# Splitting the last output tile into 512, 320, 128 and 64 columns, with the last 64 finished by ScalarE

One core of one Trainium2 chip. The metric is device microseconds (us) of one execution of the whole program, on the slowest core; there is only one core here. Smaller is better.

## The reference, cut to what matters

```python
    x = A_x                                   # 2048 x 1024, bf16
    h = x + _A_ref(_layernorm(x), ...)        # attention with a memory, 4 segments, 32 heads
    h2 = h + _B_ref(_layernorm(h), ...)       # gated MLP; its last step is the product below
    # in _B_ref:
    return jnp.einsum('bsf,fd->bsd', z1 * g, w_out)     # (2048 x 1792) times (1792 x 1024)
```

Only the very last step matters here. The product with `w_out` is made in 16 row tiles of 128 rows. Each tile sums 14 matmuls of 128 x 128 weights into PSUM, the accumulator memory, for each piece of its 1024 columns. It then adds the residual `h` and is stored.

## The kernel before: the parts that matter

The kernel lists its operations, lets a scheduler order them on each engine, and links them with semaphores. TensorE (PE in the profile) keeps the order of the program. `c3` is the product with `w_out` for one row tile:

```python
    def c3(b, tcl, parts):
        tc = 4 * b + tcl
        if parts[0][0] == 0:
            dma(HX[tc % 4][:], out2d[tc * 128:(tc + 1) * 128, :])       # h comes back, long before
        bks = [bank() for x in parts]
        for fc in range(14):
            for bk, (c0, w) in zip(bks, parts):
                mm(bk[:, 0:w], YT[b, fc][:, tcl * 128:(tcl + 1) * 128], WOUT[:, fc, c0:c0 + w], fc == 0, fc == 13)
        for bk, (c0, w) in zip(bks, parts):
            hh = HX[tc % 4][:, c0:c0 + w]
            tt(hh, hh, bk[:, 0:w], ALU.add)                             # VectorE: residual + PSUM
            dma(out2d[tc * 128:(tc + 1) * 128, c0:c0 + w], hh)          # store, issued by SP
    # ...
            for parts in ([((0, 512), (512, 512))] if (b, tcl) != (3, 3) else
                          [((0, 512),), ((512, 384),), ((896, 128),)]):
                c3(b, tcl, parts)
```

The last tile is already cut into 512, 384 and 128 columns, so that little is left to add and store when the last matmul is done.

The softmax here doesn't subtract the row's maximum and nothing guards it: scores larger than these inputs give would overflow.

## Time and profile before

| | before |
|---|---|
| time, first 3 runs, median | 796.82 us (796.44 to 797.57) |
| span of the profiled execution | 794.4 us (794.358 in the trace) |
| TensorE busy | 783.0 us, 99% |
| start of the last 512-column add | 789.02 us |
| from there to the end of the span, "the tail" | 5.34 us |

The *tail* of the last row runs from the start of the last tile's 512-column add to the end of the span. The page prints the span to 0.1 us; I take its end from the trace to a nanosecond. The lines themselves are in the prediction.

### The profile page before, as it was taken

The page shows a single profiled execution, that of the slowest core. Times are in us where ns is not written, and L with a number is a line of the kernel's source. Part 1 is how long each engine was busy: PE and PEld are TensorE (multiplying, and loading weights), DVE is VectorE, ACT ScalarE, POOL GpSimd, SP SyncE. Part 2 cuts the span into 40 slices and gives each one's busy share as a digit, 9 for nine tenths or more (in the row PEclk, how much of TensorE's full clock was granted, in tenths as well). Part 3 has the DMA queues.
Part 4 walks back from the last instruction along what each step waited for, and adds up shares of the span by engine and source line. Part 5 has one row for each costly group of instructions (what it writes and reads, how often), then busy time and mean ns, then how long its engine had stood idle before and what let it go on. Part 6 is the DMA issues. An engine that isn't in the chain of part 4 may idle for free.

```text
span 794.4 us, 11964 instructions
## 1 busy us (share of the span) xinstructions
PE 783.0 (99%) x5273; PEld 321.3 (40%) x4765; DVE 369.4 (47%) x854; ACT 290.6 (37%) x342; POOL 138.7 (17%) x266
## 2 busy tenths in 40 slices
PE   8999999999999999999999999999999999999998
PEld 3455554555554542341322314443244334424433
DVE  6784687868766686804215051132233223322322
ACT  5778887787778852132323323100000000000000
POOL 0454543444433431200001010000000000000000
PEclk9999999999999999999999999999999999999999
DMA  9756612732333657510000116703310530011001
GB/s 282 190 126 160 147 42 67 147 81 54 74 88 95 160 138 210 157 40 1 1 0 1 33 32 156 183 1 78 109 32 1 119 100 1 0 55 59 0 1 53
DMA packets 129526, 65.02 MB, mean 82 GB/s; under 512 B 96576, under 2 KB 121408, under 8 KB 129472
## 3 DMA queue, kind: packets, MB, share of 16 engines
q1 hardware_dynamic: 129472, 64.25, 32.4%
q8 instruction: 39, 0.64, 0.3%
q14 instruction: 15, 0.12, 0.1%
HBM read 32.51 MB, written 8.39 MB: 51 GB/s over the span
## 4 chain that ended last, share of the span: by engine, by line
PE 96%; DVE 2%; issue 1%; ACT 1%; DMA 0%; POOL 0%; SPq 0%
PE ps L327 78%; PE ps L328 15%; PE ps L464 3%; ACT e L473 0%; DMA xin<-in_A_x_dram 0%; DVE stats L570 0%; DVE xin L489 0%; DVE hx L495 0%; DVE pkt L498 0%; ACT hx L587 0%; PE ps L468 0%; DVE oq L495 0%; SPq L516 0%; DVE v L485 0%; ACT hx L585 0%
## 5 line engine op out<-in xcount | busy, mean ns | idle before, releaser
L327 PE MATMUL ps<-wspT,z 128*128 128x512 bf16 x878 | 193.1, 380 | 0.9
L473 ACT ACTIVATE e<-ps 128x2048 bf16<-128x2048 f32 x80 | 149.8, 1873 | 35.1 <-PE ps L464 35.1
L327 PEld LDWEIGHTS ps<-wspT,z 128*128 128x128 bf16 x896 | 87.6, 98 | 106.5 <-issue 1.0
L473 ACT ACTIVATE z<-ps 128x512 bf16<-128x512 f32 x120 | 63.1, 572 | 145.4 <-PE ps L327 140.5
L495 DVE TENSOR_TENSOR tg<-ps,brow 128x512 bf16<-128x512 f32 x56 | 38.7, 691 | 150.0 <-PE ps L327 119.7
L327 PE MATMUL ps<-hnT,win 128*128 128x512 bf16 x438 | 96.7, 379 | 0.5
L700 POOL TENSOR_SCALAR_AFFINE_SELECT e<-e 128x1024 bf16<-128x1024 bf16 (+1 forms) x80 | 77.3, 966 | 112.3 <-ACT e L473 111.9
L328 PE MATMUL ps<-win,hnT 128*128 128x512 bf16 (+1 forms) x381 | 90.0, 344 | 0.5
L570 DVE BATCH_NORM_STATS2 stats<-z 128x6 f32<-128x448 bf16 x64 | 40.1, 627 | 96.8 <-ACT z L473 95.2
L327 PE MATMUL ps<-wout,y 128*128 128x512 bf16 (+2 forms) x243 | 82.5, 367 | 0.0
L328 PE MATMUL ps<-wout,y 128*128 128x512 bf16 x210 | 79.7, 379 | 0.5
L495 DVE TENSOR_TENSOR hx<-hx,ps 128x512 bf16<-128x512 bf16 (+1 forms) x65 | 42.2, 674 | 77.2 <-PE ps L327 76.8
L327 PEld LDWEIGHTS ps<-hnT,win 128*128 128x128 bf16 x448 | 43.8, 98 | 54.2 <-issue 2.0
L327 PE MATMUL ps<-xnT,wq 128*128 128x512 bf16 x250 | 60.3, 381 | 0.4 <-issue 0.2
L327 PE MATMUL ps<-xnT,wk 128*128 128x512 bf16 (+2 forms) x249 | 57.4, 373 | 2.4 <-DVE ra L502 1.9
L327 PE MATMUL ps<-wv,xnT 128*128 128x512 bf16 x239 | 57.2, 380 | 1.4 <-DMA wv<-in_A_wv_dram 0.5
L327 PE MATMUL ps<-wo,oT 128*128 128x512 bf16 x244 | 57.1, 379 | 0.6
L327 PEld LDWEIGHTS ps<-wout,y 128*128 128x128 bf16 x252 | 24.1, 98 | 72.3 <-issue 69.1
L327 PE MATMUL ps<-win,hnT 128*128 128x512 bf16 x122 | 46.3, 380 | 0.0
L327 PEld LDWEIGHTS ps<-win,hnT 128*128 128x128 bf16 x128 | 12.5, 98 | 81.5 <-issue 80.9
L509 POOL TENSOR_SCALAR rs<-mv 128x1 f32<-128x1 f32 x44 | 10.8, 246 | 192.9 <-DVE mv L573 192.9
L327 PEld LDWEIGHTS ps<-v,e 128*128 128x128 bf16 x1280 | 40.1, 96 | 9.8 <-issue 1.7
(72 smaller groups left out, 635.6 us busy)
## 6 DMA issues: line engine op xcount, KB each, us to landing
win<-in_B_w_in_dram SPq DMA_DIRECT2D x6, 1024.0 KB, 5.4
hx<-in_A_x_dram SPq DMA_DIRECT2D x16, 256.0 KB, 3.2
out_dram<-hx SPq DMA_DIRECT2D x16, 256.0 KB, 2.6
hx<-out_dram SPq DMA_DIRECT2D x16, 256.0 KB, 2.7
out_dram<-hx SPq DMA_DIRECT2D x31, 128.0 KB, 1.7
xin<-in_A_x_dram SPq DMA_DIRECT2D x15, 256.0 KB, 5.0
wout<-in_B_w_out_dram SPq DMA_DIRECT2D x2, 1792.0 KB, 11.1
wq<-in_A_wq_dram SPq DMA_DIRECT2D x2, 1024.0 KB, 8.6
```

Of the source, the lines that this page charges most:

```text
L327: return e.matmul(out, lhsT, rhs, start=start, stop=stop)
L328: return e.add_instruction(mybir.InstMatmult(name="I-%d" % (1000000 + o.idx), engine=e.engine, ins=[e.lower_ap(rhs), e.lower_ap(lhsT)], ou ...
L464: G.op(PE, lambda e: e.matmul(o, lhsT, rhs, start=True, stop=True, tile_position=(32 * i, 0)), [lhsT, rhs], [o], n / 2.4 if last else 3.5, ...
L473: G.op(ACT, lambda e: e.activation(o, i, func, scale=scale, **kw), r, [o], ((172 if inps(i) else 224) + n_of(i)) / 1.2 + 26, prio=prio, na ...
L495: G.op(DVE, lambda e: e.tensor_tensor(o, a, b, op), [a, b], [o], vcost(o, [a, b], fast), name="tt", prio=late[0])
L509: G.op(POOL, lambda e: e.tensor_single_scalar(o, i, s, op), [i], [o], 220 if n_of(o) < 8 else 220 + 2.5 * n_of(o), name="pts1", prio=late[0])
L570: G.op(DVE, lambda e, si=si, so=so: e.bn_stats(so, si), [si], [so], (cs + 143) / 0.96, name="bn_stats", prio=late[0])
L700: G.op(POOL, lambda e: e.affine_select(d, d, pat, ALU.is_ge, 0.0, base=0, channel_multiplier=-1), [d], [d], 1270 if j else 640, name="mask")
```

## The change

The intent is a shorter tail. The last piece is halved to 64 columns. Its residual goes into PSUM by a matmul with the identity, so that nothing has to be added afterwards. ScalarE copies it out and issues its store, so that no hand-over to another engine lies between copy and store.

```diff
+    LAST = take("last", [128, 64], BF16)
...
+        last = parts[0][1] == 64
+        if last:
+            mm(bks[0][:, 0:64], IDENT[:], HX[tc % 4][:, 960:1024], True, False)
         for fc in range(14):
             for bk, (c0, w) in zip(bks, parts):
-                mm(bk[:, 0:w], YT[b, fc][:, tcl * 128:(tcl + 1) * 128], WOUT[:, fc, c0:c0 + w], fc == 0, fc == 13)
+                mm(bk[:, 0:w], YT[b, fc][:, tcl * 128:(tcl + 1) * 128], WOUT[:, fc, c0:c0 + w],
+                   fc == 0 and not last, fc == 13)
+        if last:
+            act(LAST[:], bks[0][:, 0:64], ACTF.Copy)
+            dma(out2d[tc * 128:(tc + 1) * 128, 960:1024], LAST[:], eng=ACT)
+            return
...
-                          [((0, 512),), ((512, 384),), ((896, 128),)]):
+                          [((0, 512),), ((512, 320),), ((832, 128),), ((960, 64),)]):
```

## The prediction

> **What bounds the kernel now.** I read the page's busy line and its chain first, to see which engine sets the end:
>
> ```profile
> span 794.4 us, 11964 instructions
> PE 783.0 (99%) x5273; PEld 321.3 (40%) x4765; DVE 369.4 (47%) x854; ACT 290.6 (37%) x342; POOL 138.7 (17%) x266
> ...
> PE 96%; DVE 2%; issue 1%; ACT 1%; DMA 0%; POOL 0%; SPq 0%
> ```
>
> TensorE (PE) is busy for 99% of the span and 96% of the chain that ends last, so the kernel is one unbroken stream of matmuls. The change touches only the last of 16 row tiles of the output, after 785 us. Everything before should stay as it is, so the whole question is the tail. For that I read the timeline from 785 us on, one engine at a time (columns: start us, us, engine, line, operation, count). The vector engine (DVE):
>
> ```profile
> 789.02 0.69 DVE L495 TENSOR_TENSOR hx<-hx,ps 128x512 bf16<-128x512 bf16 x1 [1.95 <-PE ps L327]
> 791.29 0.55 DVE L495 TENSOR_TENSOR hx<-hx,ps 128x384 bf16<-128x384 bf16 x1 [1.58 <-PE ps L327]
> 792.08 0.29 DVE L495 TENSOR_TENSOR hx<-hx,ps 128x128 bf16<-128x128 bf16 x1 [0.23 <-PE ps L327]
> ```
>
> These three adds evict the pieces of 512, 384 and 128 columns; each starts when its piece's fourteenth matmul is done, so their starts are a clock for PE. Next PE's last piece, and the two last store issues of the DMA queue:
>
> ```profile
> 791.09 0.94 PE L327 MATMUL ps<-wout,y 128*128 128x128 bf16 x14
> ```
>
> ```profile
> 791.87 0.33 SPq L516 DMA_DIRECT2D out_dram<-hx  x1
> 792.39 0.33 SPq L516 DMA_DIRECT2D out_dram<-hx  x1
> ```
>
> The DVE add ends at 792.08 + 0.29 = 792.37, its store is issued 0.02 to 0.03 us later, and then nothing runs but that store. Its time to landing is in the list of DMA issues (KB each, us from issue to landing):
>
> ```profile
> out_dram<-hx SPq DMA_DIRECT2D x31, 128.0 KB, 1.7
> ...
> out_dram<-hx SPq DMA_DIRECT2D x1, 96.0 KB, 1.6
> out_dram<-hx SPq DMA_DIRECT2D x1, 32.0 KB, 1.5
> ```
>
> So the last store lands at 792.39 + 1.5 = 793.89, and the remaining 794.36 - 793.89 = 0.47 us (span 794.4) are the end of the program. After PE's last matmul the tail is therefore add 0.29, issue hop 0.03, store 1.5, end 0.47. Of these the change can alter only the first three and when PE finishes.
>
> **What the skill says.** (1) The Trainium skill, "TensorE: Matmul & The Clock Gate", section "Wait — 56ns, not 53.3ns?", gives a warm pitch of N/2.4 ns plus about 2.5 ns, never under about 25 ns. The trace agrees: the fourteen 128-column matmuls above are (0.94 - 0.22)/13 = 55 ns apart (0.22 is one matmul's row), and in the attention part sixteen of 33 columns, each with its own weights, are (0.56 - 0.18)/15 = 25 ns apart:
>
> ```profile
> 299.99 0.56 PE L327 MATMUL ps<-v,e 128*128 128x33 bf16 x16
> ```
>
> (2) "ScalarE: Activation LUTs", section "What ACT_TABLE_LOAD costs", gives an activation with immediate scale and bias 186 ns plus 0.833 ns per column, 239 ns at 64. The trace's PSUM copies are quicker than that (mean ns behind the comma), so I use them:
>
> ```profile
> L473 ACT ACTIVATE qk<-ps 128x256 bf16<-128x256 f32 x16 | 5.3, 383 | 0.0
> ...
> L473 ACT ACTIVATE qk<-ps 128x384 bf16<-128x384 f32 x1 | 0.5, 490 | 1.0 <-PE ps L327 1.0
> L473 ACT ACTIVATE qk<-ps 128x128 bf16<-128x128 f32 x1 | 0.3, 272 | 0.0
> ```
>
> (3) The same page, section "Table sets: the hidden batching unit", says that cheap functions such as copy and identity are in every set. The trace agrees: only three table loads in all, though copies stand among exponentials and GELUs. So I count no table load. (4) "DMA: Bandwidth & Descriptors", section "Issuing engines are not separate DMA queues": a DMA that ScalarE issues runs on the same 16 engines, and issuing elsewhere saves only the sequencer's time. No ScalarE-issued transfer is in this trace, so that term is unverified here.
>
> **The change part by part.**
>
> *PE.* Before, the last tile is 14 x (512, 384, 128). The DVE starts give the pitch at 384: (791.29 - 789.02)/14 = 162 ns, against 160 + 2.5 by the rule; 128 is 55.8 by the rule, in line with the 55 read above. For 320 columns the rule gives 133.3 + 2.5 = 135.8 ns and for 64 columns 26.7 + 2.5 = 29.2 ns. After, the two pieces beyond 512 become three: 14 x (135.8 + 55.8 + 29.2) = 3.09 us plus one identity matmul of 0.03 = 3.12 us; before they take 14 x (162.5 + 55.8) = 3.06 us. Column work is equal, and the 15 additional matmuls cost 14 x 2.5 ns + 29 ns = 0.06 us. All of it is on the path: PE ends 0.06 us later.
>
> *Eviction.* DVE 289 ns at 128 columns is replaced by a ScalarE copy of 64. Its rows fall by (490 - 272)/256 = 0.85 ns per column, so 64 columns cost 272 - 54 = 218 ns: 0.07 us saved. The residual needs no time of its own, as it is in PSUM already. The hand-over from PE costs the same: in the timeline the median from a matmul's modelled end to the start that waited for it is 38 ns on both engines. ScalarE's last work before is over at 503 us, so it is free.
>
> *Issue.* Before: DVE to SP hop 0.03 us. After: the issue on ScalarE waits for its own copy's semaphore, which I also take as 0.03 us. The SP queue still stores the 320 and 128 pieces. The 128 piece's add should start near 791.70, end at 791.99, and its SP issue take 792.02 to 792.35. The ScalarE issue would come at 792.08 + 0.06 + 0.22 + 0.03 = 792.39, just after, so they don't overlap. That is the same moment as the last issue now.
>
> *Store.* 16 KB instead of 32. From 96 to 32 KB the landing time falls from 1.6 to 1.5, about 2 ns per KB, so 16 KB gives 1.47: 0.03 us saved.
>
> *Sum.* +0.06 - 0.07 + 0.00 - 0.03 = -0.04 us. The change trades one thing for another almost exactly. Against it stands a first-time cost of an issue from ScalarE: the first nine loads on the SP queue took a median of 0.43 us to issue against 0.33 at the end, so I allow an estimated +0.1 us. Net +0.06 us on 796.82: 796.9 us.
>
> *What does not move.* The new 128-byte tile fits in the first free region (6400 bytes, of which six 1024-byte tiles took 6144), so the other buffers only shift by 128 bytes and none changes region. The PE order is the program's, and the operations before the last tile keep theirs.
>
> **The rivals.**
>
> *A: the intended gain.* The author counts on a shorter tail: a smaller copy and store, no engine change between copy and issue. At best the issue hop vanishes (-0.03), the store lands in 1.35 (-0.15) and the copy takes 0.19 (-0.10): -0.2 us net of PE, so 796.6. For it: the tail is serial. Against it: landing time hardly depends on size in the rows above (128 KB 1.7, 32 KB 1.5), so halving a small store buys little.
>
> *B: ScalarE's queue is slower.* A DMA issued from an engine that has issued none might take 0.5 us or more to issue, or land later because its queue is fresh. +0.2 to +0.6 us: 797.0 to 797.4. For it: nothing in the profile shows such an issue, and the start of the program shows slower first issues. Against it: the skill's page says the same hardware does it.
>
> *C: small matmuls bound by weight loads.* Each matmul loads its own 128 x 128 weights. If that load set the pace and 64 columns ran at the 55 ns of 128, the last piece would cost 14 x 26 = 0.37 us more: 797.2. Against it: the 33-column run above has a load for each matmul too, and keeps 25 ns. I give it little.
>
> *D: a disturbance elsewhere* through shifted addresses or another schedule order. It would show before 785 us; I see no mechanism.
>
> **Range and chances.** All rivals lie between 796.6 and 797.4, and the three runs before spread from 796.44 to 797.57, more than any of them. So the range is set by run noise: 796.3 to 797.5. Two per cent is 16 us, seven times everything after PE's last matmul (2.3 us), so removing the whole tail wouldn't reach it: within 2% at 0.985.
>
> **What would show it.** Right: the timeline identical up to the last tile; the 320-column add starting near 790.92 and the 128 one near 791.70; fourteen or fifteen 64-column matmuls about 29 ns apart; the ScalarE copy starting near 792.14 and taking about 218 ns; its issue near 792.39; span 794.3 to 794.6. Wrong: a ScalarE issue of over 0.5 us, or starting over 0.1 us after the copy's end (B); a landing under 1.4 us (A); a 64-column pitch above 40 ns (C); a table load before the copy; or any difference before 785 us (D).

## More of the kernel before

At the start of the program, 11 warm-up matmuls on zeros (`N_WARM = 11`) run while the first loads arrive.

The tail leaves out whatever happened in the 789 us before it.

## The result and the profile after

The changed kernel takes 796.41 us (median of 6 runs, 796.05 to 796.88). The kernel before, in the same rounds and the first three runs together, takes 796.72 (796.27 to 797.57). Ratios here are the mean time of one kernel's fast runs over the mean of the other's of the same rounds, so they are not quite the ratio of the medians. This ratio is 0.9994, with a 95% interval from 0.9981 to 1.0007: the same. (A run counts as fast unless it is over 1.5% above the quickest of its kernel. Every run here that has a verdict is fast, those with a short dip of the clock, of which more below, included.)

In the profiled execution the span is 794.7 us, longer than the 794.4 before. The page of the changed kernel, its busy line and its chain:

```profile
span 794.7 us, 11997 instructions
...
PE 783.0 (99%) x5288; PEld 321.9 (41%) x4780; DVE 369.3 (46%) x854; ACT 290.9 (37%) x343; POOL 139.0 (17%) x266
...
PE 95%; DVE 1%; issue 1%; DMA 1%; ACT 1%; SPq 0%; POOL 0%
```

TensorE has the same busy time, 15 matmuls more and 15 weight loads more (PEld, 4780 against 4765): 30 of the 33 instructions that the trace has more are TensorE's, a number to remember. The timeline of the tail, first VectorE, then TensorE, then ScalarE, each in its own fence (start us, us, engine, line, operation, count):

```profile
789.31 0.69 DVE L495 TENSOR_TENSOR hx<-hx,ps 128x512 bf16<-128x512 bf16 x1 [1.95 <-PE ps L327]
791.21 0.49 DVE L495 TENSOR_TENSOR hx<-hx,ps 128x320 bf16<-128x320 bf16 x1 [1.21 <-PE ps L327]
791.99 0.29 DVE L495 TENSOR_TENSOR hx<-hx,ps 128x128 bf16<-128x128 bf16 x1 [0.29 <-PE ps L327]
```

```profile
791.79 0.19 PE L327 MATMUL ps<-hx,ident 128*128 128x64 bf16 x1
791.82 0.57 PE L327 MATMUL ps<-wout,y 128*128 128x64 bf16 x14
```

```profile
792.43 0.22 ACT L473 ACTIVATE last<-ps 128x64 bf16<-128x64 f32 x1 [289.58 <-PE ps L327]
792.68 0.38 ACTq L516 DMA_DIRECT2D out_dram<-last  x1
```

The 512-column add starts 0.29 us later than in the profile before, so 0.29 us were lost before the changed part was reached. Counted from that add, all goes as worked out: the adds at 1.90 and 2.68 us, the 64-column matmuls (0.57 - 0.19)/13 = 29 ns apart, the copy at 3.12 us and of 0.22 us, its store issued at 3.37 us. What was not foreseen is in the stores. (A store is *issued* by SP or ScalarE, which takes some tenths of a microsecond, and it has *landed* when its data have arrived; landing times count from the start of the issue.) SP's last two issues, and then the list of issues of the tail (KB each, us from issue to landing):

```profile
791.72 0.33 SPq L516 DMA_DIRECT2D out_dram<-hx  x1
...
792.31 0.51 SPq L516 DMA_DIRECT2D out_dram<-hx  x1
```

```profile
out_dram<-hx SPq DMA_DIRECT2D x1, 80.0 KB, 1.8
out_dram<-hx SPq DMA_DIRECT2D x1, 32.0 KB, 1.7
out_dram<-last ACTq DMA_DIRECT2D x1, 16.0 KB, 1.5
```

The 128-column store takes 0.51 us to issue instead of 0.33, and the two SP stores land in 1.8 and 1.7 us, where 96 and 32 KB took 1.6 and 1.5 before. ScalarE's store is still the last to land, at 4.91 us after the add, where the last one before landed at 4.86. The tail is 5.39 us, 0.05 longer than before. So three questions: what holds the stores up, why the time nevertheless came out 0.3 us lower, and whether the parts of the change are worth anything by themselves.

### The profile page after: what moved, and what is told of

Its sections match the earlier page's. It is cut to its first block, busy times and chain, and to the rows that moved or that the text cites. A ratio compares the mean times of both kernels' runs of the same rounds, so it can differ in the third digit from the quotient of the medians.

```text
span 794.7 us, 11997 instructions
## 1 busy us (share of the span) xinstructions
PE 783.0 (99%) x5288; PEld 321.9 (41%) x4780; DVE 369.3 (46%) x854; ACT 290.9 (37%) x343; POOL 139.0 (17%) x266
## 4 chain that ended last, share of the span: by engine, by line
PE 95%; DVE 1%; issue 1%; DMA 1%; ACT 1%; SPq 0%; POOL 0%
PE ps L327 78%; PE ps L328 15%; PE ps L464 3%; DMA wv<-in_A_wv_dram 1%; ACT e L473 0%; DVE stats L570 0%; SPq L516 0%; DVE pkt L498 0%; DVE hx L495 0%; DVE xin L489 0%; DVE oq L495 0%; DVE v L485 0%; POOL e L700 0%; POOL ra L505 0%; DVE qk L485 0%
## 5 line engine op out<-in xcount | busy, mean ns | idle before, releaser
L327 PE MATMUL ps<-wout,y 128*128 128x512 bf16 (+3 forms) x257 | 82.5, 356 | 0.0
```

The source lines that it names most:

```text
L327: return e.matmul(out, lhsT, rhs, start=start, stop=stop)
```

## The experiments

Because time can't resolve a tenth of a microsecond here, the tail of the profile is the main measure, and time is a check.

### The kernel before, again

No edit.

> The kernel before against itself. I use the tail, the time from the start of the final tile's 512-column add to the end of the span: 5.34 us in the profile before, 5.39 us in the profile after. Theory N (the 0.3 us between the medians is run noise): the ratio of this identical kernel also strays by up to 0.0010 from 1, its interval includes 1, single runs spread over 1 us, and the tail repeats at 5.34 +- 0.03. Theory R (the change really gains 0.3 us somewhere): the ratio is 1.0000 +- 0.0002, so that 0.9994 stands out from it.

Ratio of the kernel before to itself: 0.9999, interval 0.9985 to 1.0013. Tail 5.35 us. The tail repeats to 0.01 us, while the time does not: one of these 6 runs took 798.34 us, the other five 796.12 to 796.56. In the 11 runs of before beside it, four took 798.08 to 798.50 and seven 795.67 to 796.79. All five long ones have a mean granted clock of 0.998 and all short ones 1.0. So a ratio of 0.9994 is well inside what a kernel does against itself, by the interval. The ratio alone doesn't decide it: 0.9999 is what theory R had expected too.

### The changed kernel, again (twice)

No edit.

> The changed kernel unaltered, more rounds on the same chip as the kernel before against itself. Theory N: ratio within 0.0006 of that other ratio, interval including 1, tail 5.39 +- 0.03, so 0.05 longer than before. Theory R: ratio 0.9993 to 0.9997 with an interval that excludes 1.

Ratio 0.9993, interval 0.9980 to 1.0007, so the interval includes 1. But the tail was 5.75 us, not 5.39 +- 0.03. SP and ScalarE in the timeline of this run, and its issues:

```profile
791.85 0.76 SPq L516 DMA_DIRECT2D out_dram<-hx  x1
...
792.22 0.38 ACTq L516 DMA_DIRECT2D out_dram<-last  x1
```

```profile
out_dram<-hx SPq DMA_DIRECT2D x1, 80.0 KB, 2.1
out_dram<-hx SPq DMA_DIRECT2D x1, 32.0 KB, 2.2
```

Same instructions at the same distances up to SP's last issue, which now takes 0.76 us; the 32 KB store then lands in 2.2 us. My second theory, of a fixed 0.05, fell here. Leaving out the runs with a clock below 1.0, the mean is 796.23 us for five runs of the changed kernel and 796.15 for seven of before on the same chip: the sign turns round. The advantage of the changed kernel in the ratio comes from having had none of the long runs.

A third profile, after the cause below had been formed:

> The changed kernel unaltered, a third profile. Its tail was 5.39 and 5.75 us. Theory F (a race of one instruction fetch with the stores): a fetch at 2.1 to 2.3 us after the 512-column add again, SP's second-last issue again over 0.4 us, tail between 5.38 and 5.85, varying with how long the fetch holds its engine. If the collision were an accident of the first two runs: issue 0.33, tail 5.34.

Tail 5.61 us, SP's last issue 0.86 us. So the hold-up is in all three profiles of the changed kernel, with tails of 5.39, 5.75 and 5.61 us, on average 5.58, which is 0.24 us above before.

### The last store from SP

```diff
-            dma(out2d[tc * 128:(tc + 1) * 128, 960:1024], LAST[:], eng=ACT)
+            dma(out2d[tc * 128:(tc + 1) * 128, 960:1024], LAST[:])
```

> The changed kernel with its last store issued by SP instead of ScalarE. In the changed kernel's profile the SP queue's store of the 128-column piece took 0.51 us to issue where others take 0.33, and landed in 1.7 us where 1.5 was seen. Theory O (the two issues overlap and slow each other): with one queue both issues take 0.33 us, the last store is issued 3.37 us after the 512-column add starts, lands in 1.48 us, and the tail is 5.32 to 5.34 us, 0.05 to 0.07 below the changed kernel. Rival (ScalarE's queue costs nothing, the slow issue was chance): tail 5.39 +- 0.02.

Tail 5.74 us; SP's last two issues take 0.70 and 0.43 us. Neither side was right. There is no ScalarE store here, and the slow issue is still there, so it isn't two queues meeting. Here the slow issue delays the last store directly, which waits behind it on the same queue and is issued 3.75 us after the add instead of 3.37.

### The pieces alone

```diff
-                          [((0, 512),), ((512, 384),), ((896, 128),)]):
+                          [((0, 512),), ((512, 320),), ((832, 128),), ((960, 64),)]):
```

This edit is on the kernel before: no identity matmul, no ScalarE.

> Pieces 512, 320, 128, 64 alone: VectorE adds every residual and SP issues every store, no identity matmul. From the adds of 384 and 128 columns (553 and 289 ns) the 64-column add takes 223 ns, as long as the ScalarE copy, and PE ends 0.03 us sooner. My sum: add starts 3.09 us after the 512-column add, ends 3.31, issue 3.34, landing 1.48, end 0.47: tail 5.29 us, 0.10 below the changed kernel and 0.05 below before. If ScalarE's part of the change was worth its cost, the tail is above 5.39.

Tail 5.47 us instead of 5.29. The add was as worked out (0.22 us, at 3.09), but SP's last two issues took 0.43 us each, and even the 512-column store of the tail landed in 3.5 us where it takes 1.7 elsewhere. So neither the identity matmul nor ScalarE is the cause. What these kernels share is a longer TensorE program. The list of DMA queues on the pages of before and after (packets, MB, share of 16 engines):

```profile
q8 instruction: 39, 0.64, 0.3%
```

```profile
q8 instruction: 40, 0.66, 0.4%
```

One more packet of 16 KB on a queue of kind "instruction". Cut to the last 6.7 us of the changed kernel, the queue view shows that the fortieth fetch is there:

```profile
q1 hardware_dynamic: 598, 0.39, 18.4%
q10 hardware_dynamic: 144, 0.02, 1.6%
q8 instruction: 1, 0.02, 0.9%
```

In the same stretch of the kernel before there is no line for that queue. The packets' records in the trace place the fetch 2.11 to 2.56 us after the 512-column add in the five profiles so far with the 64-column piece, for 0.93 to 1.26 us. In all five the fetch is under way while the 320-column store is being issued (2.42 to 2.75). In two of them its record ends before the packets of that store begin, at 3.25.

The Trainium skill has the matter on a page that I hadn't read for the prediction: "Runtime: NRT & Kernel Launch", section "Instruction fetch mechanics", says that an engine's instructions arrive in blocks of 16 KiB, 256 instructions, and that the sequencer (the part of an engine that reads its instructions) drives a DMA queue of its own to fetch the next block. The trace agrees in size (39 packets, 0.64 MB), and in pace: the fetches start about every 250 TensorE records. The same section calls the cost of a block border mostly hidden. Whether that holds here is what the next runs test.

### The fetch moved early

```diff
-    for k in range(N_WARM):
+    for k in range(N_WARM - 4):
         mm(PS[:, 7, :], ZERO[:, 0:128], ZERO[:], True, True)
+    for k in range(68):
+        mm(PS[:, 7, 0:32], ZERO[:, 0:128], ZERO[:, 0:32], True, True)
```

The changed kernel is otherwise untouched; its TensorE program is longer by 64 instructions at the far end from the tail.

> The changed kernel, but 4 of the 11 warm-up matmuls at the very start become 68 of 32 columns, so that the TensorE program has 64 instructions more before the tail. In the profiles so far a 16 KB instruction fetch starts every 256 TensorE instructions or so; in the three kernels with the 64-column piece one starts 2.1 to 2.2 us after the 512-column add, in the kernel before none does. Theory F (that fetch holds up the 320-column store and with it the SP queue): with it moved about 7 us earlier no fetch is in the last 5 us, SP's issue of the 128-column store is back from 0.51 or 0.76 to 0.33 us, the 320-column store lands in 1.65 us, and the tail, from the start of the 512-column add to the end, is 5.30 to 5.35 us instead of 5.39 and 5.75. Rival S (rows of 640 and 128 bytes, or borders off a 256-byte multiple, are slow to store): nothing changes, SP's issue stays over 0.45 us.

SP and ScalarE in the timeline of this run, and its issues:

```profile
791.95 0.33 SPq L516 DMA_DIRECT2D out_dram<-hx  x1
...
792.32 0.37 ACTq L516 DMA_DIRECT2D out_dram<-last  x1
```

```profile
out_dram<-hx SPq DMA_DIRECT2D x1, 80.0 KB, 1.6
out_dram<-hx SPq DMA_DIRECT2D x1, 32.0 KB, 1.5
```

The issue is back at 0.33 us, the landings at 1.6 and 1.5, and the tail is 5.34 us, as before the change. The rows of 640 and 128 bytes are not slow. The fetch now starts 5.8 us ahead of the 512-column add. The time is no different from before (ratio 1.0006, 0.9992 to 1.0020).

A smaller dose tells the meeting apart from the mere presence of a fetch. Here one warm-up matmul becomes 17 of 32 columns, 16 instructions more:

> The changed kernel with only 16 TensorE instructions more at the start (one warm-up matmul becomes 17 of 32 columns), so that the fetch of the tail comes some 8 matmul pairs sooner, by 1 to 1.7 us. Theory F: a fetch is still among the last 5 us, but at 0.4 to 1.3 us after the 512-column add, so it is over before the 320-column store's packets begin at 3.25; SP's issue is 0.33 us and the tail 5.33 to 5.36. If it were the mere presence of a fetch, or of TensorE's longer program, that costs: tail above 5.38 again.

The queue view of the last 5.9 us of this run, and its issues:

```profile
q8 instruction: 1, 0.02, 1.4%
```

```profile
out_dram<-hx SPq DMA_DIRECT2D x1, 128.0 KB, 2.0
out_dram<-hx SPq DMA_DIRECT2D x1, 80.0 KB, 1.6
```

The fetch is in the tail, 0.15 us after the add (a little earlier than expected) and 1.37 us long. It now meets the 512-column store, which lands in 2.0 us instead of 1.7, and nobody waits for that one. The 320-column store is clear, SP's issue takes 0.33, the tail is 5.34 us. So what a fetch costs depends on which store it meets.

The other direction, 4 warm-up matmuls fewer (`N_WARM = 7`):

> The changed kernel with 4 warm-up matmuls fewer (7 for 11), so 4 TensorE instructions fewer ahead of the tail. 16 more had moved the fetch 2.0 us earlier, so 4 fewer move it some 0.1 to 0.5 us later, to 2.3 to 2.7 us, nearer to the 320-column store's packets. Theory F: tail 5.5 to 5.9 us, as long as or longer than the unaltered kernel; or, if the page border falls past the last instruction, no fetch and 5.34. In no case a fetch there and a tail under 5.37.

The fetch didn't move visibly: it started at 2.19 us, inside the 2.11 to 2.56 that the same place gave before, so its start isn't fixed to better than some 0.4 us. SP's issue took 0.59 us and the tail was 5.48, just under the expected 5.5. The one firm claim, no fetch at that place with a tail under 5.37, held. Over all 14 profiles with the four pieces, those reported below included, the count is clean: in the six with a fetch that starts at 2.11 to 2.56 us, SP's issue of the 128-column store takes 0.43 to 0.86 us; in the eight without, it takes 0.33. The start of the last packet of the 320-column store, against the tail, in us from the add, by the packets' records:

| run | fetch starts, lasts | last 320-column packet | SP's next issue | tail |
|---|---|---|---|---|
| fetch moved early | none in the tail | 3.60 | 0.33 | 5.34 |
| 16 instructions more | 0.15, 1.37 | 3.60 | 0.33 | 5.34 |
| changed, first profile | 2.20, 0.97 | 3.61 | 0.51 | 5.39 |
| 4 instructions fewer | 2.19, 1.03 | 3.70 | 0.59 | 5.48 |
| last store from SP | 2.20, 1.13 | 3.81 | 0.70 | 5.74 |
| changed, second | 2.12, 1.26 | 3.86 | 0.76 | 5.75 |
| pieces alone | 2.11, 0.93 | 3.94 | 0.43 | 5.47 |
| changed, third | 2.56, 0.93 | 3.97 | 0.86 | 5.61 |

The later the 320-column packets end, the longer SP's next issue, in all rows but the one of the pieces alone. There the packets of the 512-column store were late too (the last at 3.70, where 2.02 is usual), so more than one store was held up. Nor does the tail follow SP's issue alone: in the second and third profile SP's 128-column store lands last, at 5.21 and 5.07 us, in the first and in the one with 4 instructions fewer it is ScalarE's, at 4.91 and 5.00. Why an issue waits for the packets of the store before it (a full queue in one of the 16 DMA engines, presumably the one that carries the fetch) is argued, not shown.

### The other two versions without the fetch

The same edit of the warm-up, on the version with the last store from SP and on the one with the pieces alone.

> The last store on SP as in the run before (tail 5.74 us, SP's issues 0.70 and 0.43 us), with the same 64 more TensorE instructions at the start. Theory F: both issues 0.33 us, last store issued 3.37 us after the 512-column add, tail 5.29 to 5.34. Rival S: tail above 5.5.

> The four pieces alone, all on VectorE and SP (tail 5.47 us with the fetch), with the fetch moved early. Theory F: issues 0.33 us each, the last at 3.34 us, tail 5.27 to 5.32, the shortest of all and below the kernel before by 0.05; its time is then within run noise of before, as 0.05 of 797 us can't be seen. Rival S: 5.47 again.

Tails of 5.37 both, down from 5.74 and 5.47, so the fetch had cost 0.37 and 0.10 us there. But both are 0.03 to 0.05 above what I had expected, and above before. The last issue on SP takes 0.43 us, not 0.33, in both, and also in the two versions with the fetch. In all four it starts 0.04 us after the end of the issue before it. The 18 traces bear this out: of 1732 SP issues that start at most 0.06 us after the end of the one before, none took less than 0.41 us, while the stores of the tail with 0.18 us or more between them take 0.33, unless the fetch meets them or two are issued at once. (Those 1732 are mostly loads of other shapes, so it is a pattern, not a test.) In the second of the two versions the issue also starts 0.06 us after its add has ended, because SP is busy until 3.33. Here lies what ScalarE's queue is good for: an issue right behind another on SP is slow, and ScalarE's first one, at 0.37, is not slower than that. The timed one of the two, the pieces alone, has ratio 0.9997 (0.9984 to 1.0009).

### The identity matmul and ScalarE, with the old pieces

The changed kernel's path for the last piece, with the pieces of before:

```diff
-                          [((0, 512),), ((512, 320),), ((832, 128),), ((960, 64),)]):
+                          [((0, 512),), ((512, 384),), ((896, 128),)]):
-        last = parts[0][1] == 64
+        last = parts[0][1] == 128
```

with 64 and 960 replaced by 128 and 896 where the piece is named.

> The kernel before with its pieces of 512, 384 and 128 columns, only the last with the identity matmul, the ScalarE copy and the ScalarE store. It adds 2 or 3 TensorE instructions, so I expect no fetch in the tail. PE ends 0.056 later, the copy of 128 columns takes 278 ns against the add's 289, its issue 0.38 (as the first one on ScalarE did) against 0.33, landing 1.55 against 1.50: tail 5.34 + 0.06 - 0.01 + 0.05 = 5.44 (5.40 to 5.47). If ScalarE's queue were as quick as SP's: 5.39.

Tail 5.43 us, no fetch in it. The copy took 0.28, the issue 0.37 and the landing 1.53 us, about as expected. So with pieces of equal size ScalarE's path costs 0.08 us more than VectorE and SP: the identity matmul 0.06, and ScalarE's issue and landing the rest.

### ScalarE's queue used once before

```diff
-            dma(out2d[tc * 128:(tc + 1) * 128, c0:c0 + w], hh)
+            dma(out2d[tc * 128:(tc + 1) * 128, c0:c0 + w], hh, eng=ACT if (b, tcl, c0) == (3, 1, 512) else SP)
```

on the changed kernel with the fetch moved early.

> The changed kernel with the fetch moved early, and one earlier store (the second half of row tile 13) issued from ScalarE too, some 12 us before the end. Without that the issue on ScalarE took 0.37 us against SP's 0.33. Theory W (the first issue of a queue is slow): the last one takes 0.33 us and the tail falls from 5.344 to 5.30. Rival (ScalarE's issue is simply 0.04 us longer, and no part of the tail): 0.37 us again and tail 5.34 +- 0.02.

> The run with the fetch moved early and ScalarE's queue used once before, again, now timed: tail 5.28 +- 0.02, so 0.06 below before and 0.11 to 0.47 below the changed kernel; the time within noise of before (ratio 0.999 to 1.001), because runs at full clock spread over 1 us at the start of the program.

ScalarE's last issue in the timeline of the first of the two, and its landing:

```profile
792.05 0.34 ACTq L516 DMA_DIRECT2D out_dram<-last  x1
```

```profile
out_dram<-last ACTq DMA_DIRECT2D x1, 16.0 KB, 1.4
```

The issue takes 0.34 instead of 0.37 us and the store lands in 1.43 and 1.44 instead of 1.49 us, and the tail is 5.28 and 5.29 us in two profiles, 0.05 to 0.06 below before. The first-use cost that I had allowed for (0.1 us) is there, and measures about 0.05 us from issue to landing. With 5 timed runs the ratio to before is 1.0002 (0.9990 to 1.0014): not to be seen in time.

### The best of the parts

The pieces alone, all added by VectorE, no identity matmul, the last store from a ScalarE queue used once before, the fetch moved early:

> Four pieces all added by VectorE, no identity matmul, the last store from a ScalarE queue used once before, the fetch moved early. The 64-column add ends at 3.31 us after the 512-column add (as in the run of pieces alone with the fetch early), SP's last issue is over at 3.33, so ScalarE's issue at 3.34 meets nothing; it takes 0.34 and lands in 1.45, end 0.46: tail 5.25 +- 0.03, the shortest. If the two queues' issues do collide so close together, it is above 5.34.

Tail 5.26 us, the shortest, 0.08 below before. In time it is not seen: ratio 1.0010 (0.9998 to 1.0022), with four of its six runs at a clock of 0.998. The two runs at full clock took 796.02 and 796.20 us, against a mean of 796.45 for ten of before. Whether the altered warm-up makes the clock dip more often is open. Over the five timed kernels with that edit 9 of 26 runs dipped; the counts per kernel range from none of 5 to 4 of 6, which is too few to say.

### Two issues at once

A store cut into two of 64 rows, on SP and ScalarE at the same moment, first on the changed kernel with the fetch moved early, then on the kernel before. Two further lines of the edit, left out here, drop the second store's wait for the first:

```diff
-            dma(out2d[tc * 128:(tc + 1) * 128, 960:1024], LAST[:], eng=ACT)
+            dma(out2d[tc * 128:tc * 128 + 64, 960:1024], LAST[0:64], eng=ACT)
...
+            dma(out2d[tc * 128 + 64:tc * 128 + 128, 960:1024], LAST[64:128])
```

> A try to beat both: the changed kernel with the fetch moved early, and its last store of 128 rows cut into two of 64 rows, one issued from ScalarE and one from SP at the same moment. If the issue and the 0.87 us from issue to the first packet grow with the rows, each half issues in about 0.2 us, first packets come at 4.05 instead of 4.24 us and the tail is 5.15 to 5.28. If they are fixed, or the two issues get in each other's way, the tail is 5.34 to 5.45.

> The kernel before with nothing changed but its last store of 128 rows by 128 columns, cut into two of 64 rows, SP and ScalarE. As in the run with the split on the changed kernel: tail 5.15 to 5.28 if issue grows with rows, 5.34 to 5.42 if not. In time neither can be told from the kernel before by its runs, which spread over 1 us at full clock.

Tails of 5.96 and 5.99 us, worse by 0.6 and outside both of my expected ranges. The two issues of the second run, and their landings:

```profile
793.50 0.56 SPq L516 DMA_DIRECT2D out_dram<-hx  x1
...
793.50 0.58 ACTq L516 DMA_DIRECT2D out_dram<-hx  x1
```

```profile
out_dram<-hx SPq DMA_DIRECT2D x1, 16.0 KB, 1.8
out_dram<-hx ACTq DMA_DIRECT2D x1, 16.0 KB, 2.1
```

Each issue takes 0.56 to 0.58 us, with half the rows of one that takes 0.33 alone. (In the first run SP's half also starts right behind an earlier issue of SP's; in the second 0.18 us lie between.) So SP and ScalarE seem to get in each other's way when they issue at the same moment. No run issued the two halves one after the other, so a cost of the 64 rows themselves isn't excluded. Nor does every overlap cost: in the second profile of the changed kernel ScalarE's issue lies wholly within SP's slow one (3.00 to 3.76 us) and takes 0.38. In the changed kernel the two are 0.04 us clear of each other once the fetch is gone. The ratios are 1.0020 (1.0006 to 1.0033) and 1.0013 (1.0000 to 1.0025). The first has three dips in five runs; at full clock the two kernels are 0.8 and 0.7 us above before, on means of 2 and 4 runs against 8, in keeping with the loss of 0.6.

### Where the spread of the time comes from

The traces answer this without a further run. The order of VectorE's operations is the same in all kernels here up to the last tile, so each can be set against its own start in another trace. The offsets from the profile of before move about until some 25 us (59 in three of the runs), and then settle: from 26 to 785 us at least 716 of the 807 operations, in every other trace, keep one offset within 0.01 us, and the rest stray for a while and come back to it. This settled offset is -0.34 to +1.11 us in the profiles at full clock. TensorE at the start, in the profile of before and in that of the old pieces on ScalarE's path:

```profile
9.55 2.12 PE L327 MATMUL ps<-wv,xnT 128*128 128x512 bf16 x9
```

```profile
10.06 2.12 PE L327 MATMUL ps<-wv,xnT 128*128 128x512 bf16 x9 [0.93 <-DMA wv<-in_A_wv_dram]
```

The second waited 0.93 us for the load of `wv`. Its 512-column add in the last tile comes at 789.52 us, 0.51 after that of before: the same 0.51 as here. The run with +1.11 (the split store on the kernel before) waited 1.51 us at the same place. In 12 of the 13 other profiles at full clock this group of nine matmuls starts as much later or earlier than before's, within 0.02 us, as the whole execution lies in the end (the last store on SP with the fetch moved early is the exception). So where an execution lies is as a rule settled within its first 10 us, in the two named by the wait for a load, and the rest follows at a fixed distance. The long runs begin there too. The profile of the split store on the changed kernel fell on one (windows of that run: us, length, busy time of PE, PEld, DVE, ACT and POOL, granted clock, DMA share, GB/s):

```profile
10.00:14.00 4.00, 4.00 (x22) 1.90 (x20) 2.25 (x5) 1.38 (x3) 0.00 (x0) 0.63 1.10 365
14.00:788.00 774.00, 773.85 (x5285) 314.97 (x4689) 357.43 (x831) 284.14 (x329) 136.86 (x256) 1.00 0.32 78
```

The clock was granted at 0.63 on average between 10 and 14 us, and at 1.00 from there to 788 us. That execution had waited 1.39 us for `wv` just before, and its 512-column add came at 791.17 us, 2.16 after that of before. In the four profiles with a dip the group of nine starts 0.7 to 1.2 us later than before's and takes 2.86 to 3.31 us instead of 2.12, so the slow clock accounts for about half of the 1.4 to 2.2 us. What sets a dip off stays open: a longer wait, the 1.51 us above, went without one.

## Why the prediction was right or wrong, point by point

- **What bounds the kernel.** Right. TensorE is at 99%, and two per cent were out of reach.
- **TensorE's part.** Right to 0.01 us. The last tile's adds came 1.90 and 2.68 us after the first (expected 790.92 and 791.70 against 789.02), the 64-column matmuls 29 ns apart. Rival C, a weight-load bound, is out.
- **The copy.** Right: 0.22 us at 3.12 us, without a table load.
- **The issue.** The moment was right, 3.37 us after the add. But "they don't overlap" rested on SP's issue taking 0.33 us, and in the three profiles of the changed kernel it took 0.51, 0.76 and 0.86. This is the step that failed, and with it "What does not move" and the path: in two of the three profiles the last store to land is SP's 128-column one, and not ScalarE's. I had looked at addresses and at the order of operations, and not at the number of TensorE instructions. 15 matmuls with their 15 weight loads carried the TensorE program over one more block border, near its end. The fetch that follows met the 320-column store, and the tail rose by 0.05, 0.41 and 0.27 us. Shown by edits of the warm-up that leave the tail's instructions as they are and move the fetch: without it there, the issue took 0.33 again and the tail was 5.34. How the fetch holds up a store stays open.
- **The store.** A term mis-sized. I expected 1.47 us for 16 KB from ScalarE. It took 1.54, 1.63 and 1.48 in the three profiles of the changed kernel, 1.49 without the fetch, and 1.43 to 1.44 from a queue used before. The allowance of 0.1 us for a first issue on ScalarE was right in kind, with about 0.05 us measured, but its ground was not: the first nine loads of SP, which took 0.43 us to issue, follow one another within 0.06 us, and issues that close take at least 0.41 us anywhere in the traces.
- **The sum.** -0.04 plus 0.1 made +0.06. Without the fetch the tail is 0.00 longer than before, with a queue used before 0.05 to 0.06 shorter, with the fetch 0.24 longer on average. The mechanism was complete but for the fetch.
- **The rivals.** A, the intended gain, is right in direction and a third in size: -0.06 us, and only once the fetch is out of the way and the queue has been used. B, a slower queue, holds for the first use only, at about 0.05 us and not 0.2 to 0.6. D, a disturbance elsewhere, is the one that came true in another form: I looked for it before 785 us and through addresses, and it came within the tail and through the length of the program.
- **The time and its range.** I expected 796.9, so slightly above before. The median came at 796.41, inside the range, but 0.31 below the median of the six runs of before, and the profiled span of 794.7 lay just above the expected 794.3 to 794.6. The direction was wrong, and the step that failed is the base: 796.82, a median of three runs, was taken as good to 0.06 us, without asking what "run noise" is made of. It has two parts: the start of the program, waits for loads among it, which put the profiles at full clock -0.34 to +1.11 us from that of before, and a dip of the clock at the same place, which comes on top of a late start; such runs take some 2 us longer. The changed kernel's 11 timed runs had no run above 797 us, while 4 of 11 of before on one chip had. At full clock on that chip the changed kernel is 0.08 us slower, on means of 5 and 7 runs. So nothing in the lower time is shown to belong to the change; that the changed kernel would dip less often isn't supported by anything found.

## What to carry to other kernels

When a change is worth less than the spread of a kernel's runs, measure it in the trace from a landmark just ahead of it, and take more than one profile, for here the same kernel gave 5.39 and 5.75 us. A change adds instructions as well as work: count on which side of a 256-instruction border the tail of the busiest engine falls, since a fetch that meets a critical store cost more here, 0.24 us on average, than the whole change was to gain. Before splitting a last store, see that the issues don't start together, nor right behind one another on one queue, and use a queue once before it is needed (worth 0.05 us here).

## What the Trainium skill lacked or had wrong

- "Runtime: NRT & Kernel Launch", section "Instruction fetch mechanics": it has the 16 KiB blocks and the queue of their own, and the trace agrees (39 and 40 packets). It calls the cost mostly hidden. Not in a tail: the fetch lengthened SP's next issue from 0.33 to as much as 0.86 us and the tail by 0.05 to 0.41 us. The page doesn't say that a fetch holds up ordinary stores.
- "DMA: Bandwidth & Descriptors", section "Issuing engines are not separate DMA queues": it says that issuing from several engines saves only the sequencer's time. Issued at the same moment from SP and ScalarE, two stores of half the rows took 0.56 to 0.59 us each to issue, against 0.33 for a whole one alone, and the tail grew by 0.6 us. With 0.38 us between the starts of two whole stores there was no such loss.
- No page that I read has the cost of the first use of a queue (0.37 against 0.34 us to issue, 1.49 against 1.43 us to land, on ScalarE).
- "TensorE: Matmul & The Clock Gate", section "Back-to-back issue gap", has about 81 ns for a stream of 128-column matmuls with a weight load each. Here it is 55 to 56 ns, and 29 ns at 64 columns.
- "ScalarE: Activation LUTs", section "What ACT_TABLE_LOAD costs": its formula gives 239 ns for the copy of 64 columns and 293 ns for 128; from PSUM they took 224 and 277 ns.
